# A decayed linear attention with a gated MLP on one core: all MLP units four chunks wide, and each output sum in a PSUM tensor of its own

## The chip, the cores and the metric

One NeuronCore of a Trainium2 chip runs the whole program. It has five engines, each with an instruction queue of its own that it works through in order: TensorE (matmuls; PE in the profile, PEld its weight loads), VectorE (DVE), ScalarE (ACT), GpSimd (POOL) and SyncE (SP), which here issues nearly all DMA transfers. Matmul results go to PSUM, eight banks of 2 KB for each partition; everything else lives in SBUF. The metric is the device time of one execution, in microseconds (us).

## What is computed

```python
def _attn_ref(q, k, v, alpha):                 # 4 batches, 8 heads, 768 steps, head size 48
    for t in range(S):
        state = alpha[:, :, t, :, None] * state + np.einsum('bhd,bhe->bhde', k[:, :, t], v[:, :, t])
        y[:, :, t] = np.einsum('bhd,bhde->bhe', q[:, :, t], state)

def _moe_ref(x, w_in, w_out):                  # x: 3072 x 384, w_in: 384 x 2048, w_out: 2048 x 384
    h = x @ w_in
    sp = np.where(h > 20.0, h, np.log1p(np.exp(np.minimum(h, 20.0))))
    g = h * np.tanh(sp)
    return (g @ w_out).astype(np.float32)
```

The attention's y, heads side by side, is the x of the MLP. The weights arrive as 64-bit floats.

## The kernel before, in words

**Chunks.** 64 steps of two batches are a chunk: 128 rows of x. There are 24 chunks, numbered in time, even ones for the first pair of batches and odd ones for the second, so chunk n needs the state of chunk n − 2. `attention(n)` makes one chunk. VectorE scans the decays (`rest` L485, `qka` L498) and scales k and q with them; none of that needs PSUM. Then a chain goes through a pair of PSUM banks: TensorE transposes k (L520), ScalarE copies that out (`ks` L524), TensorE multiplies q with the state (L530) and k with q (L536), VectorE masks (L544), TensorE multiplies with v (L549) and forms the update of the state (L559), ScalarE and VectorE split x into a high and a low part (L578, L584; for chunks 0 to 3 TensorE and ScalarE do the low part, L590, L598), and the update is added to the state (L615 on VectorE, L613 on ScalarE for chunks 0 and 1). With that the bank pair is free again. Six small DMA transfers, the moves (L604), put the rows of two heads in their places in x. All but those that ScalarE issues for chunks 0 and 1 go through SP.

Most chunks use the bank pair `att_at`. Chunks 1, 3 and 5 (`SLOT`) use banks 2 and 3 of `sums_at`, so that two chunks can be under way.

**Units.** A unit is one of the 16 tiles of the hidden width (`f`) for `nt` neighbouring chunks. Nine matmuls up (L706: three parts of 128 rows, each as high × high, high × low, low × high) give `h`; ScalarE and VectorE work out the gate in eight instructions (L714 to L740), and three matmuls down for each chunk (L770) add to the chunk's output sum, which has a PSUM bank, one of four. `h` has two buffers. `SEGMENTS` lists which chunks take which tiles in what order: before, 28 units of two chunks (chunks 0 to 7 in pairs, tiles up to 4 or 6) and 18 of four for the first eight chunks, then 64 of four. Where a group of chunks leaves its banks before tile 15, its sums are put aside (`stash` L794) and later added (L786, L801). x lies in two tiles (`xs`), each with room for four chunks, so chunks 8 to 11 overwrite 0 to 3 once the last unit that reads those is through, and so on.

**Weights.** Each of the 16 weight tiles is loaded once (`ws` L334), made into a 32-bit word on VectorE (three instructions, L346 to L356), and split into two parts by ScalarE with TensorE (tiles 0 to 3, L381, through sum bank 0) or GpSimd (L372). It is loaded a second time for a check (`wc` L400) that ScalarE makes (L409, L412). Both loads share two buffers.

**PSUM.** `sums_at` is one tensor of four banks, `att_at` one of two, `h` two of one bank each.

**Order.** `Plan.order` makes a fixed order for every engine. Each task has a cost, a delay until its result is there (`COST`) and a key that says how urgent it is; the planner takes, over and over, the task that can begin first by its own clock, and among equals the lowest key. A task can begin when its needs are done, its buffers are free and its engine is free. Once built, the order stands: an engine waits for the next instruction in its queue, even if later ones could go. To keep TensorE at work at the start, the planner puts up to 150 fill matmuls (L829) where its clock says that TensorE is idle, up to `IDLE_UNTIL`.

Of the kernel before, what the change touches and what calls it, by code (L numbers as in the profile page):

```python
# [9 lines left out]
F32 = mybir.dt.float32  # L10
# [17 lines left out]
DM, FF = 384, 2048  # L28
P = 128
C = 128  # L30
L = 64
NCH = S // L
NPAIR = H // 2
NSEG = 2 * NPAIR
R = 112
NFF = FF // P
NK = DM // P
QKA = 2 * NSEG * L + NSEG * (L + 1) + 1

SEGMENTS = [(0, 2, 0, 5), (2, 2, 0, 7), (0, 2, 5, 7), (4, 2, 0, 7)]  # L40
SEGMENTS += [(6, 2, 0, 7), (4, 4, 7, 11), (0, 4, 7, NFF), (4, 4, 11, NFF)]
SEGMENTS += [(c0, 4, 0, NFF) for c0 in range(8, 24, 4)]

X_TILES = [4, 4]
bank_of = lambda n, nt: n % nt
X_AT = [(n // 4 % 2, n % 4) for n in range(24)]
SLOT = {1: "pair", 3: "pair", 5: "pair"}
NT_MOST = max(s[1] for s in SEGMENTS)
BUFS = {
    "qka": 2, "v": 2, "rest": 1, "probs": 2, "att": 1, "kb": 1, "x3": 1, "stage": 2, "lead": 2,  # L50
# [10 lines left out]
CHECK_FROM = 45.0  # L61
CHECK_STEP = 2.0
FILLS = 150
IDLE, IDLE_UNTIL, IDLE_BANK = 12.34567, 24.0, "o1"
PARTED = 3
DUE_SHIFT = {}
W_SHIFT = {5: -2, 7: -2, 15: -1}
# [3 lines left out]
MOVER = lambda n, s, r: "ACT" if n < 2 and r else "SP"  # L71

STOP_AT = 1e9
ENGINES = ("PE", "DVE", "ACT", "POOL", "SP")
BEGIN = {"PE": 3.0, "DVE": 4.3, "ACT": 2.2, "POOL": 4.2, "SP": 1.2}

# [16 lines left out]
class Plan:  # L93
# [34 lines left out]
    def order(self):  # L128
# [10 lines left out]
        def ready(t):  # L139
            at = 0.0  # L140
            for x in t.needs:
                if x.begin is None:
                    return None
                at = max(at, x.begin + x.late)
            for x in t.behind:
                if x.begin is None:
                    return None
                at = max(at, x.begin)
            want = {}
            for u in t.uses:  # L150
                if not u.taken:
                    i = want.get(u.tag, 0)
                    q = self.queues[u.tag]
                    if heads[u.tag] + i >= len(q) or q[heads[u.tag] + i] is not u:
                        return None
                    if len(free_slots[u.tag]) <= i:
                        return None
                    at = max(at, free_slots[u.tag][i])
                    want[u.tag] = i + 1
            return at  # L160

# [75 lines left out]
def fast_path(ctx, tc, qka, v, w, out, good):  # L237
# [53 lines left out]
    wo = const.tile([P, 2, NFF, DM], F32R, name="wo")  # L291
    xs = [const.tile([P, 2, NK, k * C], F32R, name=f"xs{i}") for i, k in enumerate(X_TILES)]

    sums_at = ps.tile([P, NT_MOST, NPAIR * C], F32, tag="sums", name="sums_at", bufs=1)
    att_at = ps.tile([P, 2, NPAIR * C], F32, tag="att", name="att_at", bufs=1)

    plan = Plan({tag: n for tag, n in BUFS.items()} | {f"o{i}": 1 for i in range(NT_MOST)})
# [30 lines left out]
    def weight(f):  # L328
# [34 lines left out]
        for m in range(2):  # L363
            hi, lo = (wo[:, z, f : f + 1, :] if m else wi[:, z, :, fs] for z in range(2))
            as_hi = lambda t, hi=hi: t.rearrange("p (s f) -> p s f", f=hi.shape[-1])
            both = lambda m=m: lead.tile[:, m].bitcast(F32)

            def upper(both=both, hi=hi, as_hi=as_hi):
                nc.scalar.activation(hi, as_hi(both()), AF.Copy)  # L369

            def lower(both=both, hi=hi, lo=lo, as_hi=as_hi):
                nc.gpsimd.tensor_tensor(lo, as_hi(both()), hi.bitcast(F32), ALU.subtract)  # L372

            k = key + 0.5 * m
            a = add("ACT", *COST["w hi"], k + 0.03, upper, [bits], [lead])
            if W_PE(f, m):
                bank = plan.buffer(W_PE_BANKS[(2 * f + m) % len(W_PE_BANKS)])

                def off(bank=bank, both=both, hi=hi, as_hi=as_hi, m=m):
                    p = bank.tile = sums_at[:, int(bank.tag[1])][:, :DM]  # L380
                    nc.tensor.matmul(p, ident, both(), start=True, stop=False)  # L381
                    nc.tensor.matmul(as_hi(p), minus_ident, hi, start=False, stop=True)

                def left(bank=bank, lo=lo, as_hi=as_hi):
                    nc.scalar.activation(lo, as_hi(bank.tile[:, :DM]), AF.Copy)

                t = add("PE", *COST["w off"], k + 0.04, off, [a], [lead, bank])
                b = add("ACT", *COST["w hi"], k + 0.05, left, [t], [bank])
            else:
                b = add("POOL", *COST["w lo"], k + 0.04, lower, [a], [lead], port=True)  # L390
            ready_w[f, m] = [a, b]
# [34 lines left out]
    def attention(n):  # L426
# [2 lines left out]
        first, last = c == 0, c == NCH - 1  # L429
        st, key = state[b], due[n]  # L430
        q_buf, v_buf, rest, x3 = (plan.buffer(z) for z in ("qka", "v", "rest", "x3"))
        if n in SLOT:
            banks, at = [plan.buffer("o2"), plan.buffer("o3")], sums_at[:, 2:4]
        else:
            banks, at = [plan.buffer("att")], att_at
        half = lambda z: at[:, :, z * NPAIR * L : (z + 1) * NPAIR * L].rearrange(
            "p a (j t) -> p a j t", j=NPAIR
        )
# [254 lines left out]
    def unit(c0, nt, f, at, ends):  # L693
# [64 lines left out]
        for j in range(nt):  # L758
# [6 lines left out]

            def down(o=o, j=j, n=n, begins=begins, end=end, bank=bank):
                if begins:
                    o.tile = sums_at[:, bank][:, :DM]
                for m, (a, z) in enumerate(((0, 0), (0, 1), (1, 0))):
                    nc.tensor.matmul(  # L770
                        o.tile, g.tile[:, a, j * C : (j + 1) * C], wo[:, z, f],
                        start=begins and m == 0, stop=end and m == 2,
                    )
# [48 lines left out]
    if FILLS:  # L822
# [2 lines left out]

        def fill():
            if spare.tile is None:
                spare.tile = sums_at[:, int(spare.tag[1])]
            nc.tensor.matmul(  # L829
                spare.tile[:, :DM].rearrange("p (j t) -> p j t", j=NK), some,  # L830
                some.unsqueeze(1).broadcast_to([P, NK, P]), start=True, stop=True,
# [261 lines left out]
```

## Time and profile before

| | us |
|---|---|
| median of three runs | 541.43 (540.56 to 549.33) |
| the profiled execution | 544.11 |
| its span, first to last instruction | 542.3 |
| TensorE busy | 506.7 |
| ScalarE busy | 397.0 |
| VectorE busy | 380.7 |

Busy times are sums over the span. Instructions of one engine follow each other in a pipeline, so a busy TensorE is not always one at its peak. A row of the timeline names start, duration, engine, line, operation, output and inputs, how many, and in brackets the idle time before it with the engine and line that ended it.

### The profile page before, as it was taken

How to read it: one execution, taken by the hardware profiler on the slowest of the kernel's cores; microseconds unless marked ns; L12 is line 12 of the kernel's file. 1: busy time of each engine (PE TensorE's matmuls, PEld its weight loads, DVE VectorE, ACT ScalarE, POOL GpSimd, SP SyncE). 2: the span in 40 equal slices, each digit the busy share in tenths (PEclk: the TensorE clock that was granted, in tenths of full speed). 3: DMA queues.
4: the chain of work that ended last, by engine and by line, in shares of the span. 5: the costliest groups of instructions: out<-in, count | busy, mean ns of one | idle time of the engine just before them, and what ended most of it. 6: DMA issues, size and time to landing. Idle time of an engine off the chain costs nothing.

```text
span 542.3 us, 13194 instructions
## 1 busy us (share of the span) xinstructions
PE 506.7 (93%) x5275; PEld 437.8 (81%) x5275; DVE 380.7 (70%) x638; ACT 397.0 (73%) x926; POOL 41.7 (8%) x36
## 2 busy tenths in 40 slices
PE   7788889989989999799999999999999999999993
PEld 4456788888879987688889988889888889899992
DVE  7857879999989778596796459874459544444450
ACT  2348578788968999599898776667775767877762
POOL 2001210153323300000000000000000000000000
PEclk9979899999999999999999999999999999999998
DMA  8755432443243366654670043220042000110002
GB/s 270 202 168 174 128 103 88 136 158 103 73 126 113 125 198 199 183 180 136 198 238 7 3 126 81 75 74 0 16 116 79 10 7 2 32 28 0 1 1 61
DMA packets 22464, 54.46 MB, mean 100 GB/s; under 512 B 4416, under 2 KB 15168, under 8 KB 22400
## 3 DMA queue, kind: packets, MB, share of 16 engines
q1 hardware_dynamic: 22112, 53.49, 32.9%
q8 instruction: 42, 0.69, 0.6%
q14 instruction: 22, 0.18, 0.1%
q10 hardware_dynamic: 288, 0.10, 0.1%
HBM read 46.50 MB, written 4.72 MB: 94 GB/s over the span
## 4 chain that ended last, share of the span: by engine, by line
PE 74%; DVE 12%; ACT 6%; DMA 3%; issue 3%; SPq 0%; ACTq 0%; DVEq 0%
PE sums_at L770 32%; PE h L706 30%; DMA qka<-in_qka_dram 3%; PE att_at L530 2%; PE sums_at L829 2%; PE att_at L549 2%; PE att_at L536 2%; DVE t L733 2%; PE sums_at L381 1%; DVE rest L485 1%; DVE y L724 1%; DVE g L740 1%; PE att_at L559 1%; PE att_at L520 1%; DVE w_lead L356 1%
## 5 line engine op out<-in xcount | busy, mean ns | idle before, releaser
L770 PE MATMUL sums_at<-wo,g 128*128 128x384 f32 x1152 | 231.9, 343 | 13.9 <-ACT osb L808 3.5
L770 PEld LDWEIGHTS sums_at<-wo,g 128*128 128x128 f32 x1152 | 199.2, 188 | 28.4 <-ACT osb L808 6.0
L706 PE MATMUL h<-xs,wi 128*128 128x512 f32 (+1 forms) x990 | 220.7, 368 | 0.6 <-DVE y L724 0.4
L706 PEld LDWEIGHTS h<-xs,wi 128*128 128x128 f32 x990 | 170.4, 189 | 27.6 <-DVE y L724 1.6
L714 ACT ACTIVATE u<-h 128x512 f32<-128x512 f32 (+1 forms) x110 | 59.4, 540 | 68.3 <-PE h L706 68.3
L740 DVE TENSOR_TENSOR g<-t,g 128x512 fp32r<-128x512 f32 (+1 forms) x110 | 71.2, 649 | 54.1 <-ACT g L737 54.0
L724 DVE SCALAR_TENSOR_TENSOR y<-u,h 128x512 f32<-128x512 f32 (+1 forms) x110 | 67.2, 613 | 43.4 <-ACT u L714 43.3
L733 DVE SCALAR_TENSOR_TENSOR t<-y,t 128x512 f32<-128x512 f32 (+1 forms) x110 | 69.3, 632 | 11.7 <-ACT t L730 11.7
L727 ACT ACTIVATE t<-t,tenth 128x512 f32<-128x512 f32 (+1 forms) x110 | 73.1, 665 | 1.9
L737 ACT ACTIVATE g<-t 128x512 fp32r<-128x512 f32 (+1 forms) x110 | 62.5, 569 | 11.7 <-DVE t L733 6.2
L720 ACT ACTIVATE t<-u 128x512 f32<-128x512 f32 (+1 forms) x110 | 63.2, 575 | 3.5 <-DVE g L740 1.5
L730 ACT ACTIVATE t<-t 128x512 f32<-128x512 f32 (+1 forms) x110 | 62.3, 567 | 0.5
L485 DVE TENSOR_TENSOR_SCAN rest<-qka,behind 112x520 f32<-112x520 f32 x24 | 31.0, 1294 | 13.3 <-DMA qka<-in_qka_dram 13.2
L372 POOL TENSOR_TENSOR wi<-w_lead,wi 128x384 fp32r<-128x384 f32 x12 | 20.3, 1696 | 131.1 <-ACT wi L369 131.1
L498 DVE TENSOR_TENSOR_SCAN qka<-qka,ahead 112x520 f32<-112x520 f32 x24 | 30.0, 1250 | 0.0
L714 ACT ACTIVATION_READ_ACCUMULATOR u<-h 128x1 f32 x110 | 21.4, 195 | 0.0
L544 DVE COPY_PREDICATED probs<-causal,att_at 128x512 f32<-128x512 uint32 x21 | 15.5, 736 | 7.4 <-PE att_at L536 7.4
L530 PEld LDWEIGHTS att_at<-qka,state 48*64 48x64 f32 (+1 forms) x640 | 11.5, 131 | 10.3 <-issue 4.5
L372 POOL TENSOR_TENSOR wo<-w_lead,wo 128x384 fp32r<-128x384 f32 x12 | 18.7, 1562 | 6.8 <-DVE t L733 4.6
L829 PE MATMUL sums_at<-ident 128*128 128x384 bf16 x59 | 14.1, 382 | 4.9 <-POOL ident masks.py:199 2.5
L530 PE MATMUL att_at<-qka,state 48*64 48x64 f32 (+1 forms) x640 | 14.2, 227 | 4.3 <-DVE state L513 1.8
L508 DVE TENSOR_TENSOR qka<-qka 112x512 f32<-112x512 f32 x24 | 17.4, 725 | 0.0
(107 smaller groups left out, 382.3 us busy)
## 6 DMA issues: line engine op xcount, KB each, us to landing
qka<-in_qka_dram SPq DMA_DIRECT2D x21, 675.9 KB, 5.3
ws<-in_wp_dram SPq DMA_DIRECT2D x16, 768.0 KB, 4.6
wc<-in_wp_dram SPq DMA_DIRECT2D x16, 768.0 KB, 4.9
v<-in_vp_dram SPq DMA_DIRECT2D x24, 192.0 KB, 3.2
out_dram<-osb SPq DMA_DIRECT2D x32, 96.0 KB, 2.2
xs<-x SPq DMA_DIRECT2D x138, 16.0 KB, 1.9
out_dram<-part SPq DMA_DIRECT2D x16, 96.0 KB, 2.3
qka<-in_qka_dram SPq DMA_DIRECT2D x2, 448.0 KB, 5.8
```

What stands on the lines that cost most here:

```text
L372: nc.gpsimd.tensor_tensor(lo, as_hi(both()), hi.bitcast(F32), ALU.subtract)
L530: nc.tensor.matmul(y[64 * a : 64 * a + wide, u, j], st[r : r + D, e : e + wide], Q()[r : r + D, j, u], start=j == 0, stop=False, skip_grou ...
L706: nc.tensor.matmul(p[:, :N], wi[:, z, s, fs], x[:, a, s], start=m == 0, stop=m == len(passes) - 1)
L714: nc.scalar.activation(wide(u), wide(h), AF.Exp, scale=-1.0, accum_out=uchk[:, at : at + 1])
L720: nc.scalar.activation(wide(t), wide(u), AF.Square, bias=1.0, scale=2.0)
L724: nc.vector.scalar_tensor_tensor(wide(y), wide(u), 0.5, wide(h), ALU.add, ALU.mult)
L727: nc.scalar.activation(wide(t), wide(t), AF.Ln, bias=tenth, scale=0.1)
L730: nc.scalar.activation(wide(t), wide(t), AF.Exp, scale=-1.0)
L733: nc.vector.scalar_tensor_tensor(wide(t), wide(y), 0.4, wide(t), ALU.mult, ALU.mult)
L737: nc.scalar.activation(g.tile[:, 0, :N], wide(t), AF.Copy)
L740: nc.vector.tensor_tensor(g.tile[:, 1, :N], wide(t), g.tile[:, 0, :N].bitcast(F32), ALU.subtract)
L770: nc.tensor.matmul(o.tile, g.tile[:, a, j * C : (j + 1) * C], wo[:, z, f], start=begins and m == 0, stop=end and m == 2,)
```

## The change

Five things change together. `SEGMENTS` has units of four chunks alone: chunks 0 to 3 take tiles 0 to 8, chunks 4 to 7 the same, then both groups tiles 9 to 15, so 32 units for the first eight chunks and 96 in all. Chunks 1, 3 and 5 no longer use the banks of the sums. `sums_at` becomes a list of four tensors of one bank. The planner counts a buffer as free for a transfer of SP only 2.5 us after its own clock has it free, so that loads come later in SP's queue, behind moves. Fills may be planned up to 45 in place of 24.

```diff
-SEGMENTS = [(0, 2, 0, 5), (2, 2, 0, 7), (0, 2, 5, 7), (4, 2, 0, 7)]
-SEGMENTS += [(6, 2, 0, 7), (4, 4, 7, 11), (0, 4, 7, NFF), (4, 4, 11, NFF)]
+SEGMENTS = [(0, 4, 0, 9), (4, 4, 0, 9), (0, 4, 9, NFF), (4, 4, 9, NFF)]
 SEGMENTS += [(c0, 4, 0, NFF) for c0 in range(8, 24, 4)]
...
-SLOT = {1: "pair", 3: "pair", 5: "pair"}
...
-IDLE, IDLE_UNTIL, IDLE_BANK = 12.34567, 24.0, "o1"
+IDLE, IDLE_UNTIL, IDLE_BANK = 12.34567, 45.0, "o1"
...
+LOAD_MARGIN = 2.5
...
-                    at = max(at, free_slots[u.tag][i])
+                    at = max(at, free_slots[u.tag][i] + (LOAD_MARGIN if t.engine == "SP" else 0.0))
...
-    sums_at = ps.tile([P, NT_MOST, NPAIR * C], F32, tag="sums", name="sums_at", bufs=1)
+    sums_at = [
+        ps.tile([P, NPAIR * C], F32, tag=f"sums{i}", name=f"sums_at{i}", bufs=1)
+        for i in range(NT_MOST)
+    ]
...
-                    p = bank.tile = sums_at[:, int(bank.tag[1])][:, :DM]
+                    p = bank.tile = sums_at[int(bank.tag[1])][:, :DM]
...
-        if n in SLOT:
-            banks, at = [plan.buffer("o2"), plan.buffer("o3")], sums_at[:, 2:4]
-        else:
-            banks, at = [plan.buffer("att")], att_at
+        banks, at = [plan.buffer("att")], att_at
...
-                    o.tile = sums_at[:, bank][:, :DM]
+                    o.tile = sums_at[bank][:, :DM]
```

The remaining line of the diff takes the fill's bank from the list in the same way. Line numbers shift by one or two.

**TensorE, at the first unit.** Before, the first unit (two chunks, `h_469`) stands right after chunk 2's product with v, and the low parts of chunk 2 and of a weight follow it:

```order
L549 MATMUL att_at<-probs_92,v_270 48x64
L706 MATMUL h_469<-xs_106,wi 128x256 x9
L590 MATMUL att_at<-x_2_479,minus_ident 112x64 x2
L590 MATMUL att_at<-xs_106,minus_ident 112x192 x2
L381 MATMUL sums_at<-w_lead_358,ident 128x384
L382 MATMUL sums_at<-wo,minus_ident 128x384
L706 MATMUL h_496<-xs_106,wi 128x256 x9
```

Now the first unit (four chunks, `h_783`) stands behind the whole attention of chunk 4, whose update (L558) ends so:

```order
L558 MATMUL att_at<-v_597,ks_699 48x48 x2
L558 MATMUL att_at<-v_597,ks_699 64x48
L705 MATMUL h_783<-xs_106,wi 128x512 x9
L705 MATMUL h_802<-xs_106,wi 128x512 x9
L519 MATMUL att_at<-ident,qka_650 128x112 x4
L705 MATMUL h_833<-xs_106,wi 128x512 x9
```

What moved is the first unit, from behind two chunks to behind five, and all fills and all weights split by TensorE now stand ahead of it.

**SP, at the moves of chunk 8.** Before, four check loads stand ahead of these moves and a fifth ahead of the load of chunk 11 (`qka_2507`); `qka_2080` is chunk 10's:

```order
L454 DMA qka_2080<-in_qka_dram 112x1545
L334 DMA ws_2101<-in_wp_dram 128x1536
L463 DMA v_2152<-in_vp_dram 128x384
L400 DMA wc_2256<-in_wp_dram 128x1536
L400 DMA wc_2275<-in_wp_dram 128x1536
L400 DMA wc_2356<-in_wp_dram 128x1536
L400 DMA wc_2393<-in_wp_dram 128x1536
L604 DMA xs_106<-x_8_2148 16x2x128 x6
L400 DMA wc_2490<-in_wp_dram 128x1536
L454 DMA qka_2507<-in_qka_dram 112x1545
```

Now (`qka_1910` and `qka_2204` are chunks 10 and 11):

```order
L402 DMA wc_1797<-in_wp_dram 128x1536
L453 DMA qka_1910<-in_qka_dram 112x1545
L402 DMA wc_1928<-in_wp_dram 128x1536
L462 DMA v_1945<-in_vp_dram 128x384
L603 DMA xs_106<-x_8_1925 16x2x128 x6
L402 DMA wc_2181<-in_wp_dram 128x1536
L453 DMA qka_2204<-in_qka_dram 112x1545
```

What moved are two of the check loads, to behind the moves.

**TensorE, the last unit's matmuls down.** With the waits of each instruction shown. Before, the first matmul of the third and of the fourth sum waits for ScalarE, which reads a sum:

```order
L770 MATMUL sums_at<-wo,g_6284 128x384 [waits Activation_49]
L770 MATMUL sums_at<-wo,g_6284 128x384
L770 MATMUL sums_at<-wo,g_6284 128x384 [waits DVE_49]
L770 MATMUL sums_at<-wo,g_6284 128x384 x3
L770 MATMUL sums_at<-wo,g_6284 128x384 [waits Activation_49]
L770 MATMUL sums_at<-wo,g_6284 128x384 x2
```

Now each sum is a tensor of its own (108 to 111):

```order
L769 MATMUL sums_at_108<-wo,g_6040 128x384 [waits Activation_49]
L769 MATMUL sums_at_108<-wo,g_6040 128x384
L769 MATMUL sums_at_108<-wo,g_6040 128x384 [waits DVE_49]
L769 MATMUL sums_at_109<-wo,g_6040 128x384 x3
L769 MATMUL sums_at_110<-wo,g_6040 128x384 x3
L769 MATMUL sums_at_111<-wo,g_6040 128x384 x3
```

What is gone are the waits ahead of the third and the fourth sum; those for the two parts of `g` stay.

## Rows read from the trace of the kernel before

**Rows 1.** The core's span and its mean granted TensorE clock.

```profile
core 0: 542.3 us, clock 0.986
```

**Rows 2.** Busy time of each engine by stage, with the number of instructions (x); then granted clock of TensorE, share of the DMA engines, GB/s. The stages end at the first unit, at the first unit on chunks 8 to 11, and at the last unit.

```profile
0.00:38.60 38.60, 30.09 (x387) 17.87 (x387) 28.99 (x45) 12.65 (x30) 2.91 (x12) 0.91 0.72 218
38.60:228.70 190.10, 174.25 (x2104) 153.55 (x2100) 159.54 (x276) 151.37 (x400) 38.79 (x24) 0.99 0.44 135
228.70:522.70 294.00, 291.68 (x2737) 257.19 (x2736) 187.58 (x307) 225.93 (x481) 0.00 (x0) 1.00 0.23 66
522.70:542.30 19.60, 10.64 (x56) 9.18 (x55) 4.55 (x10) 7.02 (x18) 0.00 (x0) 0.88 0.18 43
```

**Rows 3.** The chain of waits in order of time (start, us, what): units of two chunks, the last unit that reads chunks 0 to 3 (182.49), and the last units of four.

```profile
124.42 1.07 PE h L706 x9
125.49 1.04 PE sums_at L770 x6
...
182.49 2.08 PE h L706 x9
184.58 2.10 PE sums_at L770 x12
...
518.51 2.08 PE h L706 x9
520.59 2.10 PE sums_at L770 x12
522.69 2.08 PE h L706 x9
```

**Rows 4.** The same chain: the first matmuls of two units, with one more unit and one chunk of attention between them.

```profile
325.93 2.09 PE h L706 x9
...
337.25 2.09 PE h L706 x9
```

**Rows 5.** Timeline of VectorE and of TensorE, 182 to 237 us: the state updates of chunks 8 to 11, the scan of chunk 12, and TensorE around the first unit on chunks 8 to 11 (228.73).

```profile
186.70 0.55 DVE L615 TENSOR_TENSOR state<-att_at,state 112x384 f32<-112x384 f32 x1
...
199.46 0.53 DVE L615 TENSOR_TENSOR state<-att_at,state 112x384 f32<-112x384 f32 x1
...
210.04 0.55 DVE L615 TENSOR_TENSOR state<-att_at,state 112x384 f32<-112x384 f32 x1
...
219.61 0.55 DVE L615 TENSOR_TENSOR state<-att_at,state 112x384 f32<-112x384 f32 x1
...
225.89 1.24 DVE L485 TENSOR_TENSOR_SCAN rest<-qka,behind 112x520 f32<-112x520 f32 x1 [2.20 <-DMA qka<-in_qka_dram]
...
228.10 0.79 PE L770 MATMUL sums_at<-wo,g 128*128 128x384 f32 x3 [2.69 <-DVE part L801]
228.73 6.65 PE L706 MATMUL h<-xs,wi 128*128 128x512 f32 x27
```

**Rows 6.** Timeline of SP's transfers, 150 to 240 us: start, time from the first issue to the last, and count.

```profile
169.67 14.37 SPq L400 DMA_DIRECT2D wc<-in_wp_dram  x4
186.86 3.78 SPq L604 DMA_DIRECT2D xs<-x  x6
...
214.75 5.99 SPq L816 DMA_DIRECT2D out_dram<-part  x8
220.84 0.53 SPq L454 DMA_DIRECT2D qka<-in_qka_dram  x1
```

**Rows 7.** Groups of instructions by line and shape: busy us, mean ns of one, idle time before them and what ended it. The low part of g, for four and for two chunks.

```profile
L740 DVE TENSOR_TENSOR g<-t,g 128x512 fp32r<-128x512 f32 x82 | 56.4, 688 | 52.4 <-ACT g L737 52.3
...
L740 DVE TENSOR_TENSOR g<-t,g 128x256 fp32r<-128x256 f32 x28 | 14.8, 533 | 1.7 <-ACT g L737 1.7
```

**Rows 8.** Timeline of ScalarE and VectorE, 0 to 62 us: the last step of chunks 0, 1 and 2.

```profile
17.39 0.48 ACT L613 COPY state<-att_at 112x384 f32<-112x384 f32 x1 [1.87 <-issue]
...
31.06 0.48 ACT L613 COPY state<-sums_at 112x384 f32<-112x384 f32 x1 [2.90 <-PE sums_at L829]
...
43.65 0.53 DVE L615 TENSOR_TENSOR state<-att_at,state 112x384 f32<-112x384 f32 x1
```

**Rows 9.** Transfers (KB each, median us from issue to landing), and from the list of waits the scans' waits for qka (us in total, times, longest).

```profile
qka<-in_qka_dram SPq DMA_DIRECT2D x21, 675.9 KB, 5.3
...
xs<-x SPq DMA_DIRECT2D x138, 16.0 KB, 1.9
...
DVE rest L485 <- DMA qka<-in_qka_dram: 13.2, 13, 2.7
```

**Rows 10.** Busy times as in rows 2, for two other stretches.

```profile
60.00:180.00 120.00, 110.95 (x1213) 99.49 (x1212) 109.64 (x190) 93.56 (x253) 34.52 (x22) 0.99 0.36 113
...
29.00:36.00 7.00, 5.85 (x73) 3.73 (x74) 2.56 (x5) 2.54 (x6) 0.00 (x0) 0.51 0.59 180
```

**Rows 11.** Timeline: TensorE at a change of group, and the last unit's end on VectorE, ScalarE and TensorE.

```profile
312.80 0.79 PE L770 MATMUL sums_at<-wo,g 128*128 128x384 f32 x3 [0.67 <-ACT osb L808]
...
529.53 0.69 DVE L740 TENSOR_TENSOR g<-t,g 128x512 fp32r<-128x512 f32 x1 [0.76 <-ACT g L737]
531.60 0.49 ACT L808 ACTIVATE osb<-sums_at 128x384 f32<-128x384 f32 x1 [2.10 <-PE sums_at L770]
...
532.23 0.79 PE L770 MATMUL sums_at<-wo,g 128*128 128x384 f32 x3 [0.67 <-ACT osb L808]
...
535.37 0.20 ACT L808 ACTIVATION_READ_ACCUMULATOR osb<-sums_at 128x1 f32 x1
```

More of the change, by code (lines that the diff above doesn't have):

```diff
@@ L827, in fill @@
             if spare.tile is None:
-                spare.tile = sums_at[:, int(spare.tag[1])]
+                spare.tile = sums_at[int(spare.tag[1])]
             nc.tensor.matmul(
```

## The prediction, made before the changed kernel ran

> **What bounds the kernel now.** I read the stages first, by the busy time of each engine [rows 2]. Up to 38.6 us no unit of the gated part exists. From 38.6 to 228.7 the first eight chunks pass through all 16 weight tiles: TensorE is busy 174 of 190 us, VectorE 160. From 228.7 to 522.7 TensorE is busy 291.7 of 294.0. The tail takes 19.6. So the last 294 us are TensorE's own work, and what can be won lies in the first two stages and the tail.
>
> Then the chain of waits [rows 3]. A unit of four chunks costs 2.08 up and 2.10 down, 4.18 us together. A unit of two chunks costs 1.07 and 1.04, half of that, so TensorE pays nothing for narrow units. One chunk of attention costs TensorE 2.96: from 325.93 to 337.25 are 11.32 us, two units (8.36) and one chunk [rows 4]. The middle stage must hold 28 × 2.11 + 18 × 4.18 = 134.3 of units and some 9.4 chunks (4 to 11 and parts of 2, 3 and 12) × 2.96 = 27.8, together 162. It took 190. Thus 28 us are lost there although TensorE reads as busy: a matmul's busy time also covers its pipeline.
>
> Where it is lost shows best between 182 and 229 [rows 3, 5]. The last unit that reads the x of chunks 0 to 3 begins at 182.49, ends at 184.6, and only then may chunk 8 write its x into that tile. The four chunks then go one after another through one pair of PSUM banks. Their state updates begin at 186.70, 199.46, 210.04 and 219.61, spaced 12.8, 10.6 and 9.6, mean c = 11.0; the first unit on them begins at 228.73. TensorE had only five units (20.9) and about four chunks (11.8) to put in these 44.1 us. In the same stretch SP sent eight stores, 5.99 us, ahead of a qka load that VectorE then awaited for 2.20, and TensorE waited 2.69 for the sum join queued behind it [rows 5, 6].
>
> **The change, part by part.**
>
> *Wider first units.* 28 units of two and 4 + 9 + 5 = 18 of four become 32 of four: 133.8 us of TensorE against 134.3, nothing gained there. VectorE and ScalarE gain, since their fixed part is paid once for four chunks: one subtraction costs 533 ns for two and 688 for four, so this form alone loses 14 × (2 × 533 − 688) = 5.3 us [rows 7]. It lies beside TensorE's work, so I cost it at zero.
>
> *Later start.* The first unit now needs chunks 0 to 3, and TensorE's queue puts chunk 4's attention ahead of it too. Chunk 0 ends at 17.39 + 0.48 = 17.9 [rows 8]. Chunks 1 and 3 no longer have a second pair of banks, so 1, 2 and 3 follow in series: 3c. Of chunk 4 only the part up to its update is awaited; I estimate 5 us, near half of c, between 3 and 9. First unit: 17.9 + 32.9 + 5 = **55.8**, against 38.6. With c at 9.6 and 12.8 it is 51.7 and 61.3.
>
> *From the first unit to the first unit on chunks 8 to 11 (unit 33).* TensorE needs 32 × 4.18 = 133.8 and seven chunks (5 to 11) × 2.96 = 20.7. Two waits can come on top. Unit 10 needs chunk 7: about 2 + 3c + 9.1 = 44 after the first unit begins, where 2 is the update of chunk 4, and 9.1 the time from the last update to the first unit that uses it, as now [rows 5]; TensorE needs 9 × 4.18 + 3 × 2.96 = 46.5 by then, so no wait unless c passes 11.8. Unit 33 needs chunk 11: 2.1 + 3c + 9.1 = 44.1 after unit 25, the new last reader of chunks 0 to 3. But now seven units stand between, not five: 29.3 + 3 × 2.96 = 38.2. That is a wait of 5.9, or a little less if the moves go out sooner; I take **5**, between 0 (c = 9) and 11.4 (c = 12.8). Unit 33 begins at 55.8 + 133.8 + 20.7 + 5 = **215.3**, against 228.7: 13.4 won.
>
> *Cover of VectorE.* It was busy 29.0 + 159.5 = 188.5 us up to 228.7 [rows 2]. Even all of this, run without a gap, would end near 192, before 215. It ran 91% busy between 60 and 180 [rows 10], and 188.5 / 0.91 is 207. So it is close, but not the bound.
>
> *Loads planned behind moves.* SP keeps its 16 weight loads, 16 check loads, 24 chunks and 144 moves less those on ScalarE; only their order changes. Chunk 8's moves had four check loads ahead of them, issued between 169.67 and 184 [rows 6]; now two stand there. A move takes about 0.63 to issue and 1.9 to land, a qka load 5.3 [rows 6, 9]. On the good side the wait of 2.69 goes; on the bad side a load is up to 5.3 late for a chunk. I take nothing beyond the lower moves wait above.
>
> *One tensor for each bank.* At 312.80 TensorE waits 0.67 for ScalarE to read another bank of the same tensor, with three such changes of group after 228.7: 2.0 us, between 0 and 4 [rows 11]. At the end VectorE gives the last operand at 529.53 + 0.69 = 530.2; four sums of 0.53 each (a quarter of 2.10) could be done by 532.4 and the last result by 533.1, but banks and results alternate, each waiting for the other, until 535.6: **2.5** won in the tail. The order shows these waits gone. Tail: 19.6 − 2.5 = 17.1.
>
> *Last stage.* The transposes and scores of chunk 12 move behind unit 33, about half a chunk: + 1.5. So 294.0 + 1.5 − 2.0 = 293.5.
>
> *Fills for longer.* 126 in place of 59 before the first unit. TensorE's clock was granted 0.51 between 29 and 36, nearly all of it the lower level, 1.2 GHz, with 5.85 of 7.0 us busy [rows 10]; 2.9 us is the most that full clock there can save, and as much could be lost if a fill stands ahead of a ready matmul. I take 0, since the serial chunk chain covers either.
>
> **Sum.** 215.3 + 293.5 + 17.1 = 525.9 us of span, against 542.3 [rows 1]. The profiled execution took 544.11, 1.8 outside the span, so 527.7, which is 16.4 less. That execution stood 2.7 above the median of 541.43; against the median the forecast is **525**.
>
> **Rivals.** All of them turn on c, the time from one chunk's update to the next when only one pair of banks is there.
>
> *Faster: c falls to 9.* In the early stage a ScalarE copy waited 2.90 for TensorE's matmuls on another bank of the shared tensor, so chunk 1 ended at 31.5, and 2 at 44.2, the queue being full of such waits [rows 8]. If these are what stretched c, the start is at 49.9 (5.9 sooner) and the wait of 5 goes: **514**. Against it: in the stretch that gave 12.8 to 9.6 no chunk used that tensor.
>
> *Same: c is the longest seen, 12.8.* The start is 5.5 later, unit 10 waits 3.0, unit 33 waits 5.5 more: **539**. For it: chunk 1 to chunk 2 took 12.6 in the early stage, with two pairs; and weight preparation, which shared that stage, stays there. Against it: nothing of the gated part now shares the start.
> The Trainium skill (Perfetto Trace Analysis, Optimization Strategy) says that a gap repeating on an engine that should be saturated can mean too little SBUF or PSUM for the next tile. By that rule, giving up the second pair of banks is wrong, and the time is this 539. No row shows the early chunks on one pair, so the trace neither bears it out nor denies it; it is why this rival keeps a good chance.
>
> *Slower: late loads in series.* A load is now put behind moves, VectorE takes its queue in order, and one scan awaits the load. If every chunk from 1 on waits the full landing of 5.3, c is 16.3: start + 15.9, unit 10 + 13.5, unit 33 + 15.9, so **570**. It is slower by over 2% once 3(c − 11) twice and 3(c − 11.8) pass 27.3, that is from c = 14.3. Against it: two qka buffers, and the scans need no bank, so they can run a chunk ahead; in the run before, 13 waits for qka make 13.2 us in all, the longest 2.7 [rows 9].
>
> That the change does nothing is excluded in part: the waits on other banks and the two-chunk units are gone from the order. What may still fail is that 17 us of later start are not won back; that is the 539.
>
> **Chances.** Forecast 0.50, c near 9 0.22, c near 12.8 0.22, late loads 0.06. The range is **509 to 540**: from a little below the fast case to the 12.8 case, with 2 in 10 outside. A measurement tells about 2% from no change, 530.6 and 552.3 around the median. The forecast and the fast case lie below, save a small part: faster 0.70, same 0.24, slower 0.06.
>
> **What would show it.** First unit near 56; updates of chunks 1 to 3 11 apart; unit 10 without a wait; unit 33 near 215, with the wait ahead of it 5; 4.18 per unit with nothing between ScalarE's results and the next sum; results of the last unit following its sums without alternating. The forecast is wrong if the first unit comes after 62, if VectorE's scans show waits for qka on many chunks, or if TensorE loses more than some 10 us between units 1 and 25, where I gave it none.

## The result and the profile after

The changed kernel takes **524.38 us** (median of four runs, 522.97 to 524.85), against 542.11 for the four runs of the kernel before: ratio 0.9667, 95% interval 0.9629 to 0.9705. The forecast was 525, the range 509 to 540. The time came out nearly as predicted. The reasons did so only in part.

The span and clock of the profiled execution (522.97 us), beside [rows 1]:

```profile
core 0: 521.2 us, clock 0.993
```

Busy time by stage, in the columns of [rows 2]. The cuts are the first unit, unit 10 (the first on chunks 4 to 7), the end of the matmuls up of unit 25 (the last reader of chunks 0 to 3), unit 33 (the first on chunks 8 to 11) and the last unit:

```profile
0.00:51.90 51.90, 45.60 (x762) 28.98 (x762) 44.83 (x66) 20.26 (x50) 8.27 (x16) 1.00 0.71 220
51.90:97.40 45.50, 42.29 (x558) 36.69 (x554) 43.37 (x66) 32.19 (x71) 7.55 (x6) 0.96 0.48 155
97.40:165.30 67.90, 67.90 (x458) 60.88 (x457) 60.72 (x83) 57.07 (x120) 22.58 (x14) 1.00 0.30 96
165.30:206.60 41.30, 41.30 (x563) 36.49 (x562) 31.32 (x54) 37.02 (x85) 0.00 (x0) 1.00 0.51 152
206.60:503.50 296.90, 296.68 (x2830) 263.32 (x2829) 192.00 (x314) 232.95 (x501) 0.00 (x0) 1.00 0.25 75
503.50:521.20 17.70, 10.31 (x58) 9.48 (x56) 4.55 (x10) 7.16 (x18) 0.00 (x0) 0.89 0.19 46
```

The first unit comes 13.3 us later (51.9 against 38.6). From 97.4 to 503.5 TensorE is busy 405.88 of 406.1. Unit 33 comes 22.1 sooner than the first unit on chunks 8 to 11 did. After the first unit, TensorE waits long only in the second stage. VectorE's and TensorE's timelines there:

```profile
58.04 1.24 DVE L484 TENSOR_TENSOR_SCAN rest<-qka,behind 112x520 f32<-112x520 f32 x1 [0.92 <-DMA qka<-in_qka_dram]
...
59.90 1.38 DVE L493 TENSOR_TENSOR qka<-qka,rest 112x512 f32<-112x512 f32 x1
61.20 1.23 DVE L497 TENSOR_TENSOR_SCAN qka<-qka,ahead 112x520 f32<-112x520 f32 x1
62.35 0.69 DVE L543 COPY_PREDICATED probs<-causal,att_at 128x512 f32<-128x512 uint32 x1
```

```profile
63.10 1.03 PE L548 MATMUL att_at<-probs,v 64*64 64x64 f32 x32 [3.21 <-DVE probs L543]
63.88 1.07 PE L558 MATMUL att_at<-v,ks 64*48 64x48 f32 x32
64.88 3.16 PE L705 MATMUL h<-xs,wi 128*128 128x512 f32 x9
...
206.56 2.24 PE L705 MATMUL h<-xs,wi 128*128 128x512 f32 x9
```

The mask of chunk 5 stands in VectorE's queue behind the scans of chunk 6. TensorE waits 3.21 for it, and the unit after it takes 3.16, unit 33 in the same view 2.24. Just behind the wait the granted clock is at its lower level, which makes the 0.96 of this stage:

```profile
63.30:66.70 3.40, 3.40 (x68) 2.98 (x61) 3.40 (x7) 1.80 (x5) 0.95 (x1) 0.50 0.35 118
```

Chunks 8 to 11, VectorE's state updates, against [rows 5]:

```profile
167.27 0.55 DVE L614 TENSOR_TENSOR state<-att_at,state 112x384 f32<-112x384 f32 x1
178.37 0.55 DVE L614 TENSOR_TENSOR state<-att_at,state 112x384 f32<-112x384 f32 x1
...
189.91 0.55 DVE L614 TENSOR_TENSOR state<-att_at,state 112x384 f32<-112x384 f32 x1
...
199.30 0.55 DVE L614 TENSOR_TENSOR state<-att_at,state 112x384 f32<-112x384 f32 x1
```

They are 11.1, 11.5 and 9.4 apart, mean 10.7 against 11.0: the chain of chunks is hardly quicker. Part of what went is in the lists of waits. Before, TensorE's matmuls into a sum waited like this (us in total, times, longest):

```profile
PE sums_at L770 <- ACT osb L808: 3.5, 6, 0.7
PE sums_at L770 <- DVE part L801: 3.5, 3, 2.7
PE sums_at L770 <- ACT part L794: 2.3, 3, 0.9
PE sums_at L770 <- DVE part L786: 1.4, 2, 0.7
```

These are 10.7 us; the program waits as for one tensor, whichever bank is read. After, no matmul of L769 (L770 before) waits for a reader of a sum; the scans' waits for `qka` fell from 13.2 [rows 9] to this:

```profile
DVE rest L484 <- DMA qka<-in_qka_dram: 7.7, 7, 2.2
```

The last unit, TensorE and ScalarE, against [rows 11]:

```profile
505.62 7.99 PE L769 MATMUL sums_at<-wo,g 128*128 128x384 f32 x45
```

```profile
512.09 0.49 ACT L807 ACTIVATE osb<-sums_at 128x384 f32<-128x384 f32 x1 [1.58 <-PE sums_at L769]
...
512.61 0.49 ACT L807 ACTIVATE osb<-sums_at 128x384 f32<-128x384 f32 x1
...
513.13 0.49 ACT L807 ACTIVATE osb<-sums_at 128x384 f32<-128x384 f32 x1
...
513.65 0.49 ACT L807 ACTIVATE osb<-sums_at 128x384 f32<-128x384 f32 x1
```

The 45 matmuls run as one group, and ScalarE reads the four sums one after another, with no matmul between. The last read ends at 514.2, 10.7 after the last unit begins; before it was 13.0.

### The profile page after: what moved, and what is told of

Same layout as the page of the kernel before. It is cut to its first block, busy times and chain, and to the rows that moved or that the text cites. A ratio compares the mean times of both kernels' runs of the same rounds, so it can differ in the third digit from the quotient of the medians.

```text
span 521.2 us, 12933 instructions
## 1 busy us (share of the span) xinstructions
PE 504.1 (97%) x5216; PEld 435.8 (84%) x5216; DVE 376.8 (72%) x590; ACT 386.6 (74%) x842; POOL 38.4 (7%) x36
## 4 chain that ended last, share of the span: by engine, by line
PE 86%; DMA 6%; DVE 3%; SPq 2%; ACT 1%; issue 1%; POOL 0%; ACTq 0%; DVEq 0%; POOLq 0%
PE sums_at L769 37%; PE h L705 36%; DMA qka<-in_qka_dram 4%; PE sums_at L828 2%; PE att_at L548 2%; PE att_at L529 2%; PE att_at L535 2%; PE att_at L558 1%; SPq L603 1%; PE att_at L519 1%; DMA ws<-in_wp_dram 1%; DVE rest L484 1%; DMA xs<-x 0%; DVE qka L497 0%; ACT osb L807 0%
## 5 line engine op out<-in xcount | busy, mean ns | idle before, releaser
L769 PE MATMUL sums_at<-wo,g 128*128 128x384 f32 x1152 | 225.3, 340 | 0.2 <-DVE g L739 0.2
L705 PE MATMUL h<-xs,wi 128*128 128x512 f32 x864 | 217.3, 396 | 0.0
L769 PEld LDWEIGHTS sums_at<-wo,g 128*128 128x128 f32 x1152 | 201.8, 188 | 8.7 <-DVE g L739 0.5
L713 ACT ACTIVATE u<-h 128x512 f32<-128x512 f32 x96 | 57.2, 596 | 71.3 <-PE h L705 70.5
L739 DVE TENSOR_TENSOR g<-t,g 128x512 fp32r<-128x512 f32 x96 | 67.4, 702 | 55.3 <-ACT g L736 54.9
L723 DVE SCALAR_TENSOR_TENSOR y<-u,h 128x512 f32<-128x512 f32 x96 | 65.4, 682 | 45.2 <-ACT u L713 45.1
L732 DVE SCALAR_TENSOR_TENSOR t<-y,t 128x512 f32<-128x512 f32 x96 | 66.6, 694 | 11.5 <-ACT t L729 11.2
L726 ACT ACTIVATE t<-t,tenth 128x512 f32<-128x512 f32 x96 | 69.3, 721 | 1.8
L719 ACT ACTIVATE t<-u 128x512 f32<-128x512 f32 x96 | 60.6, 632 | 4.4 <-DVE g L739 2.2
L736 ACT ACTIVATE g<-t 128x512 fp32r<-128x512 f32 x96 | 59.7, 622 | 3.8 <-DVE t L732 2.2
L729 ACT ACTIVATE t<-t 128x512 f32<-128x512 f32 x96 | 59.7, 622 | 0.5
L548 PEld LDWEIGHTS att_at<-probs,v 64*64 64x64 f32 (+1 forms) x768 | 13.5, 129 | 11.1 <-DVE probs L543 5.6
L548 PE MATMUL att_at<-probs,v 64*64 64x64 f32 (+1 forms) x768 | 16.9, 226 | 4.1 <-DVE probs L543 4.1
L523 ACT COPY ks<-att_at 128x448 f32<-128x448 f32 x22 | 11.6, 527 | 10.2 <-PE att_at L519 9.9
## 6 DMA issues: line engine op xcount, KB each, us to landing
qka<-in_qka_dram SPq DMA_DIRECT2D x2, 448.0 KB, 6.3
```

The lines of the kernel that those rows point to most:

```text
L548: nc.tensor.matmul(y[64 * a : 64 * a + wide, u, j], V()[own, h : h + wide], probs[slot][own, a, j], start=first and j == 0, stop=True, ski ...
L705: nc.tensor.matmul(p[:, :N], wi[:, z, s, fs], x[:, a, s], start=m == 0, stop=m == len(passes) - 1)
L713: nc.scalar.activation(wide(u), wide(h), AF.Exp, scale=-1.0, accum_out=uchk[:, at : at + 1])
L719: nc.scalar.activation(wide(t), wide(u), AF.Square, bias=1.0, scale=2.0)
L723: nc.vector.scalar_tensor_tensor(wide(y), wide(u), 0.5, wide(h), ALU.add, ALU.mult)
L726: nc.scalar.activation(wide(t), wide(t), AF.Ln, bias=tenth, scale=0.1)
```

## The experiments

Twelve kernels, in three groups of four. Each ratio is to the kernel before, run again beside that group (its medians were 543.19, 543.77 and 544.30), so medians of different groups may differ by a few us from that alone. A ratio is estimated from the single runs and need not be the quotient of the two medians; the changed kernel's own is 0.9667. To see where each kernel loses, I split its span into the start (to the first unit), TensorE's work from there to the start of the last unit, what is left of that stretch (idle, half clock), and the tail. The work is an estimate: the instructions that the trace has in that stretch, at 2.08 for nine matmuls up (1.07 for two chunks), 2.10 / 12 = 0.175 for one down [rows 3] and 2.96 for a chunk [rows 4], where a chunk is a 24th of all matmuls of the attention. What stands ahead of the first unit is in the start and not in the idle time, and each row comes from one execution. After: 95 × 2.08 + 1107 × 0.175 + 19.18 × 2.96 = 448.1. Before: 28 × 1.07 + 81 × 2.08 + 1107 × 0.175 + 21.54 × 2.96 = 455.9.

| kernel | median | ratio, 95% interval | start | work | idle | tail | span |
|---|---|---|---|---|---|---|---|
| before | 542.1 to 544.3 | 1 | 38.6 | 455.9 | 28.0 | 19.8 | 542.3 |
| the change | 524.38 | 0.9667 [0.9629, 0.9705] | 51.9 | 448.1 | 3.5 | 17.7 | 521.2 |
| one tensor again | 533.33 | 0.9822 [0.9789, 0.9856] | 53.9 | 448.1 | 10.2 | 18.7 | 530.9 |
| no load margin | 527.23 | 0.9721 [0.9671, 0.9770] | 52.5 | 448.1 | 7.9 | 17.7 | 526.2 |
| fills to 24 | 525.74 | 0.9683 [0.9648, 0.9718] | 53.9 | 448.1 | 3.9 | 18.7 | 524.6 |
| old units | 520.95 | 0.9588 [0.9554, 0.9623] | 31.8 | 456.7 | 13.8 | 17.7 | 520.0 |
| only the units | 536.64 | 0.9874 [0.9835, 0.9912] | 59.7 | 448.0 | 5.6 | 19.8 | 533.0 |
| only one pair | 534.26 | 0.9813 [0.9771, 0.9856] | 32.9 | 456.7 | 24.4 | 19.8 | 533.8 |
| only parted sums | 524.86 | 0.9614 [0.9565, 0.9663] | 31.5 | 455.9 | 17.9 | 18.9 | 524.2 |
| old units, earlier switch | 523.36 | 0.9620 [0.9581, 0.9658] | 31.5 | 456.7 | 15.5 | 17.7 | 521.4 |
| old units, two pairs | 523.70 | 0.9629 [0.9600, 0.9659] | 30.9 | 455.9 | 17.5 | 17.9 | 522.2 |
| new units, two pairs | 522.77 | 0.9614 [0.9584, 0.9644] | 48.6 | 448.1 | 7.0 | 17.8 | 521.5 |
| split at 10 | 522.35 | 0.9609 [0.9577, 0.9642] | 52.8 | 448.1 | 1.3 | 17.8 | 520.0 |
| split at 8 | 523.70 | 0.9634 [0.9604, 0.9664] | 52.2 | 448.1 | 4.0 | 17.8 | 522.1 |

### One part of the change undone

*The sums in one tensor again.*

```diff
-    sums_at = [
-        ps.tile([P, NPAIR * C], F32, tag=f"sums{i}", name=f"sums_at{i}", bufs=1)
-        for i in range(NT_MOST)
-    ]
+    sums_all = ps.tile([P, NT_MOST, NPAIR * C], F32, tag="sums", name="sums_at", bufs=1)
+    sums_at = [sums_all[:, i] for i in range(NT_MOST)]
```

> The changed kernel, with the four banks of the sums again in one tensor; every engine keeps its order, only waits come back. Theory: the separate tensors are worth the waits at three changes of group (2.0 us) and the alternation at the end (2.5), so about 529 us against 524.4, with the first unit still near 52 and unit 33 near 207. Rival: they also made the early stage shorter, where fills and weight splits use banks of the same tensor; then the first unit comes after 56 and the time is 533 or more. Rival: such waits are hidden; then it stays at 524 to 525.

533.33, the two intervals apart: the tensors are worth 1.6%, 8 to 9 us in the change's own order. I had 529 from theory; the rival's 533 came, though its first unit after 56 did not (53.9). The trace puts 2.0 at the start, 6.7 between and 1.0 in the tail, where a sum again waits for ScalarE's read of another (the last read ends 2.3 later after the last unit's start; what follows it is shorter in this execution):

```profile
521.93 0.79 PE L767 MATMUL sums_at<-wo,g 128*128 128x384 f32 x3 [0.67 <-ACT osb L805]
523.38 0.79 PE L767 MATMUL sums_at<-wo,g 128*128 128x384 f32 x3 [0.67 <-ACT osb L805]
```

*No load margin* (`LOAD_MARGIN = 0.0`), and *fills up to 24* as before.

> The changed kernel, planned without the 2.5 us of margin for SP's loads. Theory: SP's order hardly matters, because in the changed kernel TensorE has work up to unit 33 anyway: 523 to 527 us. Rival: loads ahead of moves hold up the chunk chains again, by about 2 us for each of chunks 5 to 7 and 9 to 11: unit 10 or unit 33 later by 5 or more, 530 us or more. Other rival: the margin costs, because loads come late (VectorE waited 7.7 us for qka in all): 521 or less.

> The changed kernel, with fills planned up to 24 us as before. Theory: the clock is granted at its lower level in a stretch before the first unit, but the chunk chain covers most of it: first unit 52 to 54, 524 to 527 us. Rival: the lower level reaches into the first units as well, and costs 5 us or more. Other rival: the fills themselves stood ahead of ready matmuls, and without them the first unit comes sooner: under 523.

527.23 and 525.74. Both intervals overlap the change's, so neither size is settled by time. For the margin the trace of one execution speaks: unit 33 comes at 214.7, 8.1 later, with 15 more matmuls down (2.6) done by then. For the fills the trace shows what I expected: the first unit comes at 53.9, 2.0 later, and in a stretch around it the clock is at its lower level, where the change, with its longer fills, has the higher one. First the kernel with fills to 24, then the change:

```profile
39.10:56.20 17.10, 10.44 (x205) 8.77 (x206) 14.57 (x20) 3.83 (x11) 4.57 (x4) 0.50 0.61 188
39.10:56.20 17.10, 14.27 (x267) 10.12 (x258) 16.20 (x24) 5.67 (x15) 4.81 (x4) 1.00 0.59 192
```

*The units of before.*

```diff
-SEGMENTS = [(0, 4, 0, 9), (4, 4, 0, 9), (0, 4, 9, NFF), (4, 4, 9, NFF)]
+SEGMENTS = [(0, 2, 0, 5), (2, 2, 0, 7), (0, 2, 5, 7), (4, 2, 0, 7)]
+SEGMENTS += [(6, 2, 0, 7), (4, 4, 7, 11), (0, 4, 7, NFF), (4, 4, 11, NFF)]
```

> The changed kernel with the old list of units (28 of two chunks, chunks 0 to 3 ending with only five units left before chunk 8 is needed); separate tensors, margin, fills and the single pair of banks stay. Theory: the units are the largest part; the stall between the last reader of chunks 0 to 3 and the first unit on chunk 8 comes back, some 10 to 12 us: 534 to 538 us. Rival: the other parts made the gain, and the units give little: 524 to 528. Rival: the single pair of banks cannot feed the narrow early units: over 542.

520.95: faster than the change, the intervals just apart. My theory, that the units are the largest part, fell. The table says where: the new units begin 20.1 later, have 8.6 of work already behind them by then, and save 10.3 of idle time: 1.2 worse in all, within the spans; the medians differ by 3.4. This is the lowest median of the study, but its interval overlaps those of most kernels with parted sums, so which of these is fastest is not settled.

### One part of the change alone

*Only the units*, *only one pair* (`SLOT = {}`), and *only parted sums*. In the last, chunks 1, 3 and 5 keep banks 2 and 3, which stay one tensor:

```diff
+    pair_at = ps.tile([P, 2, NPAIR * C], F32, tag="pair", name="pair_at", bufs=1)
+    sums_at = [
+        ps.tile([P, NPAIR * C], F32, tag=f"sums{i}", name=f"sums_at{i}", bufs=1)
+        for i in range(2)
+    ] + [pair_at[:, 0], pair_at[:, 1]]
...
-            banks, at = [plan.buffer("o2"), plan.buffer("o3")], sums_at[:, 2:4]
+            banks, at = [plan.buffer("o2"), plan.buffer("o3")], pair_at
```

> The kernel before with only the sums parted: banks 0 and 1 are tensors of their own, banks 2 and 3 one tensor, which chunks 1, 3 and 5 still use as their pair. Theory A1, the second pair did harm through waits on other banks of the shared tensor: they go here, so 543.2 - 9.0 - 9.0 = 525. Theory A2, it did harm by taking banks from the units and by its place in the order: only the 9.0 of the tensors, less what banks 2 and 3 still share, 534 to 536. If the parted sums do nothing without the rest, 543.

> The kernel before with one edit: chunks 1, 3 and 5 use the common pair of banks. The gain of all parts but the units is 543.2 - 520.95 = 22.2 us, of which the change's own order puts 9.0 on the tensors, 2.8 on the loads and 1.4 on the fills; 9.0 is left, and only this edit is left for it. Theory A, the second pair itself did harm: 534. Rival B, a second pair helps and the 9.0 comes from how the other parts act on units of two: 543 or more. Under A the second chunk's last step is no later than 28 us (31.1 before), under B it is later.

> The kernel before with only the list of units changed (32 units of four chunks); chunks 1, 3 and 5 still use banks 2 and 3 of the sums, which are one tensor, and loads and fills are as before. Theory 'the units cost and the rest pays': in the change's other surroundings the units cost 3.4 us (524.4 against 520.95), so here 543.2 + 3.4 = 546.6, between 543 and 551. Rival 'the units pay only where the rest stands in the way': the waits between units of two and the shared tensor are what stretches the middle stage, so fewer units relieve it: under 538.

Parting the sums alone gives 524.86: as much as the whole change, as theory A1 said. The planner knows nothing of tensors, so every engine's instructions stand in the same order as before; only the waits differ. That makes this run the cleanest proof here: nothing but the tensors changed, and 18.9 us went, 21 by the ratio. By stages, as in [rows 2], with 29 to 36 as in [rows 10]:

```profile
0.00:31.50 31.50, 25.88 (x386) 15.92 (x386) 26.37 (x42) 12.47 (x30) 2.85 (x12) 1.00 0.73 221
29.00:36.00 7.00, 6.53 (x98) 5.41 (x99) 5.62 (x9) 4.64 (x15) 0.00 (x0) 1.00 0.60 184
31.50:213.80 182.30, 173.50 (x2107) 155.75 (x2100) 160.45 (x278) 150.46 (x396) 38.74 (x24) 0.97 0.46 145
213.80:505.30 291.50, 290.38 (x2737) 257.46 (x2736) 188.82 (x310) 226.15 (x483) 0.00 (x0) 1.00 0.24 69
```

The first unit comes 7.1 sooner, and the stretch to the first unit on chunks 8 to 11 is 7.8 shorter (182.3 against 190.1), while the updates of chunks 8 to 11 stay 10.9 apart on average, against 11.0. How it was lost shows at chunk 1. Before, on TensorE:

```profile
21.32 0.48 PE L829 MATMUL sums_at<-ident 128*128 128x384 bf16 x2 [0.81 <-DVE probs L544]
22.38 0.69 PE L549 MATMUL sums_at<-probs,v 64*64 64x64 f32 x32 [0.58 <-ACT wi L385]
```

A fill into bank 1 waits for VectorE to mask chunk 1 in banks 2 and 3, and chunk 1's product then waits for ScalarE to read a weight out of bank 0. With parted sums the same two have no wait, and ScalarE's last step of chunk 1 begins at 25.4 in place of 31.1 [rows 8]:

```profile
20.38 0.50 PE L833 MATMUL sums_at<-ident 128*128 128x384 bf16 x2
20.97 0.69 PE L553 MATMUL pair_at<-probs,v 64*64 64x64 f32 x32
```

```profile
25.41 0.48 ACT L617 COPY state<-pair_at 112x384 f32<-112x384 f32 x1 [1.22 <-PE sums_at L385]
```

Only one pair gave 534.26 (theory A's 534; chunk 1's last step at 27.3), only the units 536.64, where the additive theory had 546.6 and its rival "under 538". So the parts overlap. Alone, against 543.77, the units win 7.1, the pair 9.5, the parted sums 18.9: 35.5, where the whole change wins 17.7. For the pair the lists of waits give a reason: TensorE's matmuls into the shared tensor waited 18.8 us in all for ScalarE or VectorE before (waits for the gate's results left out), and 6.8 where chunks 1, 3 and 5 no longer go through it. For the units they hardly do: 8 sums in place of 14 leave their banks early, but these waits only fall to 15.9, so how the units win 7.1 there stays open.

### Combinations and other splits

*The units of before, switching sooner to the last tiles of chunks 0 to 3*: `(4, 4, 7, 9), (0, 4, 7, NFF), (4, 4, 9, NFF)`.

> The changed kernel with the units of before, but chunks 4 to 7 take only tiles 7 and 8 (not 7 to 10) ahead of the last tiles of chunks 0 to 3, so that seven units in place of five follow the last reader of chunks 0 to 3. In the run with the old units from that reader to the first unit on chunk 8 were 47.4 us, of which six units (25.1) and about four and a half chunks (13.3) fill 38.4. Theory 'the chain of chunks 8 to 11 still leaves 9 us idle there': the reader comes 8.4 sooner and the idle time goes: 521 - 8 = 513, between 511 and 517. Rival 'weights': the last tile is ready at 154.0, just ahead of its first unit as it was, so units on tiles 13 to 15 come no sooner: 520 to 523.

523.36, no gain and 0.4 above the rival's range, but by the rival's mechanism: VectorE's last step on the last weight began at 160.9 (154.0 with the old list, which I had called ready), GpSimd's last step on its part for the matmuls up ended at 163.5 (159.0), and the last reader of chunks 0 to 3, the 39th unit, began at 166.6, not 8.4 sooner but 1.9 later than with the old list (164.7).

*Two pairs with parted sums*, with the old and with the new units (`pair_at` as above; chunks 1, 3, 5 or 1, 3):

> The changed kernel with the units of before and with banks 2 and 3 as one tensor, which chunks 1, 3 and 5 use as a second pair; it differs from the run with the old units (520.95) in the pair alone, and from the one with only parted sums (524.9) in the load margin and the longer fills. Theory 'the pair is worth nothing once the sums are parted': with parted sums the first unit came at 31.5 with the pair and at 31.8 without, so 521, between 519 and 523. Rival 'the pair costs by taking two sum banks from the units': 523 to 526, and then margin and fills gave nothing there. Rival 'a second pair helps': under 518.

> The changed kernel with its own units, and banks 2 and 3 as one tensor that chunks 1 and 3 use as a second pair. Theory 'serial chunks set the start': the first unit came at 51.9 with the four chunks 10.0, 10.7 and 7.2 apart; with a second pair a chunk can begin its transposes while the one before is still in its pair, so the first unit comes 3 to 8 sooner; what is won there is partly lost again at unit 10, which waits for chunk 7: 518 to 523. Rival 'the recurrence and VectorE set it, not the banks': 523 to 526. Slower than 527 if the pair takes banks that the weights' split and the fills need.

523.70 and 522.77; both intervals overlap those of their twins with one pair, so the pair is worth nothing that time can tell. With the old units the median lies in the range of the rival, that the pair costs something, and the overlap leaves that open. With the new units it brings the first unit 3.3 sooner, and unit 10 gives all of it back (97.3 against 97.4):

```profile
0.00:48.60 48.60, 43.59 (x751) 28.47 (x751) 40.60 (x62) 19.27 (x48) 5.54 (x14) 1.00 0.70 217
48.60:97.30 48.70, 43.27 (x556) 36.28 (x553) 45.45 (x68) 32.42 (x69) 9.87 (x8) 0.96 0.51 160
```

*The first two lists ending at tile 10, and at tile 8.*

> The changed kernel with the first two lists ending at tile 10 in place of 9. Theory 'two chains of chunks bound it': the first unit on chunks 4 to 7 came 45.5 after the first unit, where TensorE's own work was 40.7; one unit more in front makes that 44.9, so about 4 of the wait of 4.8 goes. But only six units in place of seven then stand between the last reader of chunks 0 to 3 and the first unit on chunks 8 to 11, so there 37.2 of work face a chain of 41.3, a new wait of 4.1: 524.4 in all, between 522.5 and 526.5, with the first wait gone from the trace and the second in it. Rival 'VectorE's work up to there is the bound, whatever the split': the first unit on chunks 4 to 7 stays 45.5 behind the first plus a whole unit, 49.7, and the time is 528.

> The changed kernel with the first two lists ending at tile 8. Theory 'two chains': the first unit on chunks 4 to 7 needs chunk 7, which comes no sooner, so it stays 45.5 (44 to 47) behind the first unit with only 36.5 of TensorE's work ahead of it, a wait of 9.0; eight units behind the last reader of chunks 0 to 3 then leave no wait there and 4.2 of slack that helps nobody: 524.4 + 4.2 = 528.6, between 527 and 531. Rival 'that wait is no chain but VectorE's backlog of unit work': with one unit less in front it comes 4.2 sooner, 41.3 behind the first: 524.4.

522.35 and 523.70: the split hardly matters, and "two chains" fell, as did its rival. Split at 8, the first unit on chunks 4 to 7 came 43.4 behind the first, between the two theories, and no new wait appeared: between those two units TensorE still has one wait only, the one at chunk 5:

```profile
62.83 1.12 PE L548 MATMUL att_at<-probs,v 64*64 64x64 f32 x32 [2.68 <-DVE probs L543]
```

Split at 10, that wait is gone and idle falls to 1.3, the least of all. The second wait that I expected did not come: unit 33 stood 44.2 behind the last reader, yet 384 matmuls down were done by then, in place of 357. Units' matmuls down lag behind the ups and fill such gaps; a count that puts each unit's downs before the next up misses this cover.

## Why the prediction came out as it did

**What bounds it: right.** The last stage was TensorE's own work and stayed so: predicted 293.5, measured 296.9. The size is off since the cut at unit 33 now leaves 27 matmuls down (384 less 357, 4.7 us) to the last stage. The 28 us that I found lost in the middle stage equal the table's 28.0 between the first and the last unit in part by chance: by the table's count 25.4 of these lie in the middle stage, 2.6 behind it.

**Where it was lost: wrong.** I put it on the chain of chunks through one pair of banks and made c, the time from one chunk's update to the next, the hinge of the sum and of all rivals. Then c stayed, 11.0 to 10.7, and 24.5 of the 28.0 went, though 5.5 of that only moved ahead of the first unit (13.3 of later start less 7.8 of work). I had also looked in the wrong stretch. Between 182 and 229, where I saw 11 us lost, the table's count has 4.7, as matmuls down of earlier units were still to do there; 13.5 were lost between 38.6 and 89.4, from the first unit to the first on chunks 4 to 7. The step that failed is the term *one tensor for each bank*: 2.0 + 2.5 = 4.5, sized from the changes of group after 228.7 and from the tail. It measured 8 to 9 in the change's order and 18.9 in the order of before, where 7.1 of it lay ahead of the first unit, a place to which I had given none. I had one of its rows at hand, ScalarE's wait of 2.90 [rows 8], and used it for a rival only. My argument against that rival, that between 182 and 229 no chunk used the tensor, overlooked the sums: their waits hold up TensorE's queue, and what stands behind them.

**Later start: too late by 3.9.** Predicted 17.9 + 3 × 11.0 + 5 = 55.8. In the timeline chunk 0 ended at 17.8, the next three steps were 9.1, 9.9 and 10.7, and chunk 4's part ahead of the unit took 4.4: 51.9. The form held; c in this stretch is 9.9.

**The waits: right in sum, wrong in place.** I gave unit 10 none and unit 33 a wait of 5. Unit 33 waited for nothing, and the 4.1 that the same prices leave unexplained from the first unit to unit 33 (154.7 measured, 150.6 of work) lie at chunk 5 (3.21, and the clock after it). So unit 33 came at 206.6, not 215.3: 3.9 from the start, 4.7 from the downs that lag, and little from the wait's size.

**Wider units: right that TensorE wins nothing.** Their 133.8 against 134.3 stood, and with the rest of the change the units cost a little more than they saved (3.4 by the medians). Without the rest they win 7.1, which I had not seen and cannot explain.

**Loads and fills: zero, not refuted.** 2.9 and 1.4, both inside the overlap. The half clock was real: with fills to 24 it holds from 39.1 to 56.2 in the change's order. The first unit came only 2.0 later, which fits the chain of chunks covering the rest.

**The tail:** predicted 2.5 less, measured 2.1 less (19.8 to 17.7 in the table); the last read of a sum comes 2.3 sooner after the last unit's start, so the term held.

**The rivals.** Neither c near 9 nor c near 12.8 came, and late loads in series did not either. The trace bears out no part of the 539 that the rule on repeating gaps (the Trainium skill, Perfetto Trace Analysis, Optimization Strategy) would give: a second pair was worth nothing with the sums parted, and the kernel with two pairs and one tensor was the slowest of all. The same page of the Trainium skill (Optimizing Tensor Performance, Matmuls) says to let independent groups of matmuls rotate through PSUM banks, so that one is read out beside the next one's matmuls. The kernel before did rotate through four banks; by its rows this was not enough while they were one tensor.

So the number was right by luck, by errors that cancel: what I gave to the chain of chunks was not won there, and what the tensors gave was taken two to four times too small.

## What to carry to other kernels

Give each PSUM bank that is written and read on its own a tensor of its own before anything else is reordered: a wait whose named releaser works on another part of the same tensor is the sign, since every later matmul queues behind it. Run each part of a change alone as well as undone; here parts that each won 7 to 19 us won 17.7 together. In an account of TensorE's time, count the matmuls that were done by each cut, since work that lags fills gaps that a chain seems to force.

## What was not expected of the hardware

In the falls of the granted clock looked at here, TensorE had waited just before, and the waits on the shared tensor were only one kind of such waits. Before, it was 0.51 between 29 and 36 us, nearly all of it the lower level, 1.2 GHz, although TensorE was busy 5.85 of these 7.0 us; ahead of the fall it had waited in short pieces, 0.81 and 0.58 in the two rows shown. With parted sums alone the same 7 us show 1.00, the higher level, 2.4 GHz. But TensorE stands some 7 us further in its order there, and the lower level comes later, during a wait of 3.93 for the mask of chunk 3:

```profile
43.07 1.13 PE L553 MATMUL pair_at<-probs,v 64*64 64x64 f32 x32 [3.93 <-DVE probs L548]
```

```profile
41.20:48.00 6.80, 4.93 (x46) 4.21 (x47) 5.56 (x10) 4.73 (x12) 2.17 (x2) 0.50 0.68 221
```

The kernel before and the one with only parted sums both have 10.2 us at the lower level ahead of the tail, so the parted sums did not win by the clock. In the change the clock falls behind the wait of 3.21 at chunk 5, and with fewer fills it falls in the start as well. There the fills stood in the gaps that TensorE otherwise spends waiting for the chunks.
